# Weights decoded beside the second part's steps, and the mixing's bias copied into PSUM by ScalarE

## The chip, the cores and the metric

One core of a Trainium2 chip. The time is the device time of one execution in microseconds, as the median of several runs of the whole kernel, from x and the weights in HBM to the output in HBM.

## What is computed

x has 4 batches of 3072 tokens with 256 features. The work goes through three layers, cut here to what matters:

```python
X  = rfft(x, axis=1)
Yr = Xr @ w_r - Xi @ w_i + b_r
Yi = Xr @ w_i + Xi @ w_r + b_i
Y  = soft_threshold(Yr, 0.01) + 1j * soft_threshold(Yi, 0.01)
y  = irfft(Y)

h  = y @ w_in                    # 256 -> 2048
z  = (h * tanh(softplus(h))) @ w_out

xk = mu_k * z + (1 - mu_k) * z_prev      # z_prev: the token before
xr = mu_r * z + (1 - mu_r) * z_prev
v  = relu(xk @ w_k) ** 2 @ w_v           # 256 -> 1024 -> 256
out = sigmoid(xr @ w_r2) * v
```

The weights w_in, w_out, w_k, w_v and w_r2 (called w_g in the kernel) arrive as 64-bit floats. The kernel reads each as two 32-bit words and rebuilds a 32-bit value from them, which it then splits into a high and a low part, so that three matmuls (high by high, low by high, high by low) give nearly full precision.

## The kernel before, in words

**The first part** (`part1`) is the transform, the mixing with w_r and w_i, the threshold and the inverse transform. It runs over 48 units, u = 0 to 47: four batches of NT = 12 groups of frequencies, t = u mod 12. A unit's matmuls on TensorE are F(u+1), the transform of the next unit (`emit_F`), M(u), the mixing (`emit_M`), and I(u-1), the inverse of the unit before (`emit_I`). M(u) fills one bank of the PSUM pool psy, which has three buffers: twelve matmuls of 512 columns, and a thirteenth that adds b_r and b_i. That one multiplies the constant tile pick (lines of ones, chosen by partition) by the tile bias. In a unit with t = 0 each of these is done in two halves of 256 columns, so there are 26. ScalarE and VectorE take the results out: `post_F` (a Copy to xh on ScalarE, a subtraction to xl on VectorE), `post_M` (a Relu on ScalarE), `post_M2` (a combined add and min on VectorE), `post_I` (a Copy to bs on ScalarE, and a store to b_dr on SP's queue). Between them VectorE does the butterflies of the long transform. These come from lists that a planner (`Background`) hands out: it adds up estimated costs against a clock, in which a unit is 1710 for F, 2770 for M and 1710 for I, and a list entry can have a unit by which it is due.

**The second part** (`part2`) runs over 24 blocks of 512 tokens with NC = 16 steps each, s = 0 to 383 and some more to drain. Step s has the six matmuls H(s) (`emit_H`, y by w_in, 128 of the 2048 features), a Mish on ScalarE a step later (`act_mish`), on VectorE the high and the low part of the result (`dve_g`, tiles gh and gl), and three steps after H the six matmuls acc(s-3) into the block's sums (`emit_acc`, with w_out). H and the other short-lived results share the PSUM pool psw with four buffers. From step 16 on the third layer of the block before runs in between, by the table PLAN: `evac` (copies of the sums), `token_mix` (one operation on ScalarE and three on VectorE for each half), `emit_K` and `post_K`, `emit_V`, `emit_R` (with a Sigmoid), `finish`. In block 0 the token mix stands at steps 19, 20, 24 and 25, the first K at step 22. Within one step every engine's instructions stand in the order in which the program emits them: on ScalarE the Mish first and then the list ax, on VectorE the two operations of `dve_g` with the list vx pushed between and behind them. An engine takes its own instructions in that order. What is left of the butterflies (`f3_ops`, halves of a batch, each loading a tile g) is put in by F3_PART2 and `Background.one`, a few operations per step.

**Decoding.** A weight comes in 25 pieces of 512 KB: eight of w_in, eight of w_out, four of w_k, four of w_v, one of w_g. A piece is a raw load (`raw_piece`, on SP's queue), then by `decode`: a0 (ScalarE, a Copy to integer and a Sign, into the tile sg), v0 (VectorE, two operations that put the magnitude together, into the tile q), a1 (ScalarE, Abs of q), v1 (VectorE, q by sg), a2 (ScalarE, the high part), v2 (VectorE, the low part; for w_out and w_k a2 and v2 are two operations of half the size). The class `Weights` is a pipeline of four stages: `vec()` moves every piece one stage on and gives v2 of the piece in stage 3, v1 of the one in stage 1 and v0 of the one in stage 0, in this order; `sca()` gives a2 of the piece in stage 2, a0 and a1 of the one in stage 0, and the next raw load. In the first part sg has two buffers, q three, and raw four.

All 25 are decoded in the first part. Five of the nine of w_k, w_v and w_g go through in units 6 to 14; the other 20 pieces in units 36 to 47, two per unit. The nine are parked in HBM (`park_piece`, the tensor w_dr), as their place in SBUF is taken until the second part, which fetches them back at its start (`fetch`, 21 loads on SP's queue).

```python
        def sca(self, depth):
            p = self.pipe
            ops = (p[2][3]() if p[2] else []) + (p[0][0]() + p[0][5]() if p[0] else [])
            return ops + [lambda: self.load(depth)]
```

In the profile most instructions stand under the line of a helper: 155 is `mm`, 152 `act`, 146 `tt`, 149 `stt`. They are told apart by their tiles: yps is M, xps F, bps I, hps H, a acc, kps K, u the result of the Mish.

Of the kernel before, what the change touches and what calls it, by code (L numbers as in the profile page):

```python
# [24 lines left out]
NB = 4  # L25
# [4 lines left out]
NT = 12  # L30
# [6 lines left out]
START = (20500, 20500)  # L37
SLACK = (2000, 3200)

NPARK = 5  # L40
PARK_AT = (6, 15)

F3_PART1 = {(1, 4): [(0, 0)], (1, 8): [(0, 1)]}
F3_PART2 = {1: (1, 0), 3: (1, 1), 5: (2, 0), 8: (2, 1), 10: (3, 0), 14: (3, 1)}


SPLIT_AT = (13, 14)
# [66 lines left out]
def tile_fft_mix_moe_channel_mix(  # L114
# [26 lines left out]
    def emit(ops):  # L141
        for e in ops:
            e()
# [12 lines left out]

    dram = pool(ctx, "dram", 1, space=bass.MemoryType.DRAM)
    b_dr = [dram.tile([2, 128, NT, 256], F32, name=f"b_dr{b}") for b in range(NB)]
    w_dr = [dram.tile([128, 2, 512], F32, name=f"w_dr{i}") for i in range(9)]
    y_dr = [dram.tile([2, 128, 24, 128], F32, name=f"y_dr{b}") for b in range(NB)]  # L160

    cst = pool(ctx, "cst", 1)
# [272 lines left out]

    raws = []

    def raw_piece(src):
        p, tag = raws[1][raws[0] % len(raws[1])]
        raws[0] += 1  # L440
        raw = p.tile([128, 512, 2], I32, tag=tag, name="raw", bufs=2)
        nc.sync.dma_start(out=raw.rearrange("p (k f) t -> p k (f t)", k=2),
                          in_=src.bitcast(I32).rearrange("(k p) f -> p k f", p=128))
        return raw

    def decode(raw, parts, scale=1.0):
        hw, lw = raw[:, :, 1], raw[:, :, 0]
        tl = {}

        def a0():  # L450
            sg = tl["sg"] = pools["st"].tile([128, 512], F32, tag="sg", name="sg")
            return [lambda: act(sg.bitcast(I32), hw.bitcast(F32), ACTF.Copy, scale=14000.0),
                    lambda: act(sg, sg.bitcast(I32), ACTF.Sign)]

        def v0():
            q = tl["q"] = pools["st"].tile([128, 512], F32, tag="q", name="q", bufs=3)
            qi = q.bitcast(I32)
            return [lambda: V.tensor_scalar(out=qi, in0=hw, scalar1=0x08000000, scalar2=3,
                                            op0=ALU.bitwise_xor, op1=ALU.logical_shift_left),
                    lambda: stt(qi, lw, 29, qi, ALU.logical_shift_right, ALU.bitwise_or)]  # L460

        def a1():
            return [lambda: act(tl["q"], tl["q"], ACTF.Abs)]

        def v1():
            return [lambda: stt(tl["q"], tl["q"], 3.4e38, tl["sg"], ALU.min, MULT)]

        def a2():
            tl["p"] = parts(tl["q"])
            return [lambda hi=hi, v=v: act(hi, v, ACTF.Copy, scale=scale) for hi, lo, v in tl["p"]]  # L470

        def v2():
            if scale == 1.0:
                return [lambda hi=hi, lo=lo, v=v: tt(lo, v, hi.bitcast(F32), SUB) for hi, lo, v in tl["p"]]
            return [lambda hi=hi, lo=lo, v=v: stt(lo, v, scale, hi.bitcast(F32), MULT, SUB)
                    for hi, lo, v in tl["p"]]

        return a0, v0, v1, a2, v2, a1

    def win_piece(i):  # L480
        raw = raw_piece(w_in[:, 256 * i:256 * i + 256])
        cs = slice(256 * i, 256 * i + 256)
        w = wt["in"]
        return decode(raw, lambda q: [(w[:, 0, :, cs], w[:, 1, :, cs],
                                q.rearrange("p (k f) -> p k f", k=2))])

    def wout_piece(i):
        raw = raw_piece(w_out[256 * i:256 * i + 256, :])

        def parts(q):  # L490
# [3 lines left out]
        return decode(raw, parts)  # L494


    parked = ([w_k[:, 256 * i:256 * i + 256] for i in range(4)]
              + [w_v[256 * i:256 * i + 256, :] for i in range(4)] + [w_g])

    def park_piece(i):  # L500
        raw = raw_piece(parked[i])
        tl = {}

        def parts(q):
            t = tl["t"] = yhl_p.tile([128, 2, 512], F32R, tag="yl", name="wp")
            return [(t[:, 0, :], t[:, 1, :], q)]
        a0, v0, v1, a2, v2, a1 = decode(raw, parts)
        return a0, v0, v1, a2, lambda: v2() + [lambda: nc.sync.dma_start(out=w_dr[i], in_=tl["t"].bitcast(F32))], a1

    def fetch():  # L510
        for i in range(4):
            nc.sync.dma_start(out=wt["v"][:, :, 2 * i:2 * i + 2, :].bitcast(F32),
                              in_=w_dr[4 + i].rearrange("p s (c f) -> p s c f", c=2))
        nc.sync.dma_start(out=wt["g"].bitcast(F32), in_=w_dr[8].rearrange("p s (c f) -> p s c f", c=2))
        for c in range(8):
            wt["k", c] = mat.tile([128, 2, 2, 128], F32R, tag="m", name="wkt")
            src = w_dr[c // 2].rearrange("p s (h k f) -> p s h k f", h=2, k=2)
            for z in range(2):
                nc.sync.dma_start(out=wt["k", c][:, z].bitcast(F32), in_=src[:, z, :, c % 2, :])

    class Weights:

# [48 lines left out]
    def part1():  # L571
        with ExitStack() as es:
# [11 lines left out]
            fm, im = {}, {}  # L584
            bias = c1.tile([128, 512], F32R, name="bias")
            pick = c1.tile([128, 2, 128], F32R, name="pick")
            zero = c1.tile([128, 64], F32, name="zero")
            As = {}

# [25 lines left out]
            def post_F(u):  # L615
# [7 lines left out]
                if t == 0:  # L623
# [5 lines left out]
                                     in_=zero[:, 0:4].rearrange("p (a o) -> p a o", o=1), func=ACTF.Copy)  # L629
                    xt[u] += (zh, zl)  # L630

            def emit_M(u):
                t = u % NT
                ps = psy.tile([128, 512], F32, tag="y", name="yps")
                xs = xt.pop(u)
                if t:
                    groups = [(slice(0, 512), ((0, 256, 0), (1, 0, 0)))]
# [4 lines left out]
                for gs, parts in groups:  # L642
                    n = gs.stop - gs.start
                    todo = []
                    for zl, lo in ((0, 0), (0, 1), (1, 0)):
                        for h in range(2):
                            w = wt["mix", h][lo]
                            for r, c0, z in parts:
                                todo.append((xs[z + zl][:, h, 128 * r:128 * r + 128], w[:, c0:c0 + n]))
                    todo.append((pick[:, 0 if t else 1, :], bias[:, gs]))  # L650
                    for i, (l, r) in enumerate(todo):
                        mm(ps[:, gs], l, r, i == 0, i == len(todo) - 1)
                yps[u] = ps


            def post_M(u):
# [69 lines left out]
            bg.add(both(z[8:], m[:4]) + m[4:])  # L726
            bg.flush()
            emit_F(0)
            post_F(0)
            bg.add(both(t0[0][1], t0[1][1]) + both(t0[0][2][:10], t0[1][2][:10]), 4)  # L730
            bg.add(both(t0[0][2][10:], t0[1][2][10:]), 8)
# [4 lines left out]
            for u in range(NU):  # L736
# [8 lines left out]
                bg.step()  # L745
                if u == NU - NT - 1:
                    wt["in"] = big.tile([128, 2, 2, 2048], F32R, tag="big", name="win")
                    todo = [lambda: win_piece(0)]
                    for i in range(8):
                        if i < 7:  # L750
                            todo.append(lambda i=i: win_piece(i + 1))
                        todo.append(lambda i=i: wout_piece(i))
                    late = [lambda i=i: park_piece(i) for i in range(NPARK, 9)]
                    wq = Weights(todo[:6] + late + todo[6:])
                    wq.load(3)
                dec = 0
                if b == NB - 1:
                    dec = 2
                elif PARK_AT[0] <= u < PARK_AT[1]:
                    dec = 1  # L760
                    if u == PARK_AT[0]:
                        wq = Weights([lambda i=i: park_piece(i) for i in range(NPARK)])
                        wq.load(2)
                bg.flush(u + 1)
                if u == 6:
                    S.activation(out=mu1, in_=mu, func=ACTF.Copy, scale=-1.0, bias=1.0)
                pe += 1710 * (u + 1 < NU)
                if u + 1 < NU:
                    emit_F(u + 1)
# [14 lines left out]
                    emit(wq.sca(2))  # L784
                if u > 1:
                    post_I(u - 2)
                if dec == 2:
                    emit(wq.vec())
                    emit(wq.sca(2))
                    bg.clock += 2100  # L790
                emit_M(u)
                pe = max(pe, x_at + 300) + 2770
                y_new = pe + 700
                if u:
                    emit_I(u - 1)
# [5 lines left out]
            while wq.busy():  # L801
                emit(wq.vec())
                emit(wq.sca(2))
            for h in range(2):
                emit(split_y(0, h)[1])
            post_M(NU - 1)
            post_M2(NU - 1)
            post_I(NU - 2)
            emit_I(NU - 1)
            post_I(NU - 1)  # L810
# [2 lines left out]
    def part2():  # L813
        with ExitStack() as es:
# [18 lines left out]
            xr = (xr_p.tile([128, 2, 512], F32R, name="xrh"), xr_p.tile([128, 2, 512], F32R, name="xrl"))  # L833
            xs = x2_p.tile([128, 1088], F32, name="x2s")[:, 0:1026].rearrange("p (h f) -> p h f", h=2)

            fetch()
            NC = 16
            h_t, u_t, gh, acc, kt = {}, {}, {}, {}, {}
            vps, rt, mix_t = {}, {}, {}
# [137 lines left out]
            for s in range(max(max(plan), max(fin_at)) + 2):  # L977
                j, c = divmod(s, NC)
                if s < NS:
                    if c == 10 and j + 1 < NBLK:  # L980
                        load_y(j + 1)
                    if j in F3_PART2 and c == 0:
                        bg.jobs.append(F3_PART2[j])
                    bg.step()
                    emit_H(s)
                ax, vx = defer.pop(s, ([], []))
# [12 lines left out]
                    act_mish(s - 1)  # L999
                for e in ax:  # L1000
                    e()
                vx = list(vx)
                bg.have = min(bg.have + FILL[0], FILL[1])

# [62 lines left out]
```

## Time and profile before

| | |
|---|---|
| median of 3 runs | 1982.79 us (1981.26 to 1983.64) |
| the profiled execution | 1981.86 us |
| its span | 1979.9 us |
| around the span | 1.96 us |
| TensorE busy (PE) | 1958.0 us, 99% |
| TensorE's weight loads (PEld) | 1686.2 us, 85% |
| VectorE (DVE) | 1141.4 us, 58% |
| ScalarE (ACT) | 929.0 us, 47% |
| mean granted clock of TensorE | 1.00 |

The first part ends and the second begins at about 327 us of the span. A row of the profile gives the line, the engine, the operation, the tile written and the tiles read; "idle before" is the time in which that engine did nothing ahead of it, and the arrow names what ended it. Matmuls overlap, so the mean duration of one is longer than the distance to the next. SPq rows are transfers issued on SP's queue; their duration is that of the issue.

### The profile page before, as it was taken

The page shows a single profiled execution, that of the slowest core. Times are in us where ns is not written, and L with a number is a line of the kernel's source. Part 1 is how long each engine was busy: PE and PEld are TensorE (multiplying, and loading weights), DVE is VectorE, ACT ScalarE, POOL GpSimd, SP SyncE. Part 2 cuts the span into 40 slices and gives each one's busy share as a digit, 9 for nine tenths or more (in the row PEclk, how much of TensorE's full clock was granted, in tenths as well). Part 3 has the DMA queues.
Part 4 walks back from the last instruction along what each step waited for, and adds up shares of the span by engine and source line. Part 5 has one row for each costly group of instructions (what it writes and reads, how often), then busy time and mean ns, then how long its engine had stood idle before and what let it go on. Part 6 is the DMA issues. An engine that isn't in the chain of part 4 may idle for free.

```text
span 1979.9 us, 25685 instructions
## 1 busy us (share of the span) xinstructions
PE 1958.0 (99%) x10084; PEld 1686.2 (85%) x10084; DVE 1141.4 (58%) x2183; ACT 929.0 (47%) x1525; POOL 13.2 (1%) x28
## 2 busy tenths in 40 slices
PE   6999999999999999999999999999999999999999
PEld 5888888888888888888888888888888888888888
DVE  8999976665654754465375445555544544444444
ACT  2422286344544554454445444444544544454455
POOL 0000000000000000000000000000000000000000
PEclk9999999999999999999999999999999999999999
DMA  9445276111011010101101001011000000000000
GB/s 279 150 138 170 70 245 200 39 32 65 22 33 54 22 44 11 54 22 33 54 22 54 1 22 54 5 33 38 22 1 22 22 11 12 22 23 1 22 11 22
DMA packets 104554, 106.66 MB, mean 54 GB/s; under 512 B 7017, under 2 KB 85489, under 8 KB 103409
## 3 DMA queue, kind: packets, MB, share of 16 engines
q1 hardware_dynamic: 104432, 105.02, 16.7%
q8 instruction: 79, 1.29, 0.3%
q14 instruction: 43, 0.34, 0.1%
HBM read 62.53 MB, written 42.47 MB: 53 GB/s over the span
## 4 chain that ended last, share of the span: by engine, by line
PE 97%; DMA 1%; DVE 1%; ACT 0%; issue 0%; SPq 0%; DVEq 0%; ACTq 0%
PE a L155 26%; PE hps L155 26%; PE v L155 14%; PE kps L155 13%; PE yps L155 7%; PE bps L155 4%; PE xps L155 4%; PE zps L155 3%; DMA a<-in_x_dram 1%; DMA w_dr<-wp 0%; DVE g L146 0%; ACT sg L152 0%; SPq L266 0%; DVE q L149 0%; ACT q L152 0%
## 5 line engine op out<-in xcount | busy, mean ns | idle before, releaser
L863 DVE CAST gh<-u 128x512 fp32r<-128x512 f32 x384 | 163.2, 425 | 747.5 <-PE a L155 598.2
L155 PE MATMUL a<-gh,wo 128*128 128x512 f32 x1536 | 536.3, 390 | 0.0
L155 PE MATMUL hps<-yh,win 128*128 128x512 f32 x1536 | 534.7, 389 | 0.0
L152 ACT ACTIVATE u<-hps 128x512 f32<-128x512 f32 x384 | 229.7, 598 | 525.0 <-PE hps L155 368.8
L155 PEld LDWEIGHTS hps<-yh,win 128*128 128x128 f32 x1536 | 288.3, 188 | 60.3
L155 PEld LDWEIGHTS a<-gh,wo 128*128 128x128 f32 x1536 | 288.4, 188 | 58.0
L155 PE MATMUL a<-gl,wo 128*128 128x512 f32 x768 | 299.9, 390 | 0.0
L155 PE MATMUL hps<-yl,win 128*128 128x512 f32 x768 | 298.8, 389 | 0.0
L155 PE MATMUL kps<-b,wkt 128*128 128x512 f32 x960 | 280.1, 390 | 0.0
L155 PE MATMUL v<-b,kh 128*128 128x256 f32 x1536 | 275.8, 281 | 0.0
L146 DVE TENSOR_TENSOR gl<-u,gh 128x512 fp32r<-128x512 f32 x384 | 263.6, 687 | 3.6
L155 PEld LDWEIGHTS v<-b,kh 128*128 128x128 f32 x1536 | 243.7, 190 | 7.6
L155 PE MATMUL v<-b,kl 128*128 128x256 f32 x768 | 215.8, 281 | 0.0
L155 PEld LDWEIGHTS kps<-b,wkt 128*128 128x128 f32 x960 | 179.1, 188 | 36.1
L152 ACT ACTIVATE ka<-kps 128x512 f32<-128x512 f32 x192 | 115.0, 599 | 185.5 <-PE kps L155 185.5
L155 PEld LDWEIGHTS hps<-yl,win 128*128 128x128 f32 x768 | 144.1, 188 | 29.9
L155 PEld LDWEIGHTS a<-gl,wo 128*128 128x128 f32 x768 | 144.5, 188 | 26.6
L146 DVE TENSOR_TENSOR kl<-ka,kh 128x512 fp32r<-128x512 f32 x192 | 132.5, 690 | 32.8 <-ACT ka L152 19.1
L155 PEld LDWEIGHTS v<-b,kl 128*128 128x128 f32 x768 | 144.1, 188 | 0.0
L152 ACT ACTIVATE ka<-ka 128x512 f32<-128x512 f32 x192 | 121.4, 632 | 6.3
L152 ACT ACTIVATE kh<-ka 128x512 fp32r<-128x512 f32 x192 | 121.4, 632 | 6.3
L146 DVE TENSOR_TENSOR g<-g 128x128 f32<-128x128 f32 (+3 forms) x272 | 107.5, 433 | 1.2
(80 smaller groups left out, 1926.8 us busy)
## 6 DMA issues: line engine op xcount, KB each, us to landing
b_dr<-bs SPq DMA_DIRECT2D x48, 256.0 KB, 2.2
g<-b_dr SPq DMA_DIRECT2D x8, 1536.0 KB, 6.8
y<-y_dr SPq DMA_DIRECT2D x48, 256.0 KB, 3.2
out_dram<-r SPq DMA_DIRECT2D x48, 256.0 KB, 2.2
y_dr<-g SPq DMA_DIRECT2D x80, 64.0 KB, 1.6
w_dr<-wp SPq DMA_DIRECT2D x9, 512.0 KB, 5.9
a<-in_x_dram SPq DMA_DIRECT2D x8, 512.0 KB, 6.2
y_dr<-g SPq DMA_DIRECT2D x32, 128.0 KB, 1.9
```

Source lines behind the costliest of these rows:

```text
L146: V.tensor_tensor(out=o, in0=a, in1=b, op=op)
L152: S.activation(out=o, in_=i, func=f, **kw)
L155: T.matmul(out=o, lhsT=l, rhs=r, start=start, stop=stop, **kw)
L863: return [lambda: V.tensor_copy(hi, u), lambda: tt(lo, u, hi.bitcast(F32), SUB)]
```

## The change

Two things. The weights that were parked are decoded in the second part, together with five pieces of w_out: 14 pieces, one entering at every second step from step 0 on (DEC_STEPS). Their `vec()` goes to the front of that step's list vx, their `sca()` into the next step's list ax. Their working tiles lie in the tile g, which is free there: one slot for sg, three for q, two for raw. The butterfly jobs of batch 1 move from steps 16 and 48 to 34 and 50. In the first part 11 pieces are left, one per unit from unit 34 on. w_dr is gone.

And b_r and b_i are no longer added by a matmul: the bank of M(u+1) is filled at the top of unit u by a ScalarE Copy from one of two SBUF tiles called full, and M's first matmul adds to what is there. The first three units still use a matmul, which now comes ahead of the others. The two tiles full are made once, by two matmuls and two copies behind F(0). At the end of the first part the split of y(0) moves behind post_M2(47). The planner's cost of M falls from 2770 to 2550.

```diff
-NPARK = 5
-PARK_AT = (6, 15)
+NWO = 3
+DEC_STEPS = range(0, 34, 2)
-F3_PART2 = {1: (1, 0), 3: (1, 1), 5: (2, 0), 8: (2, 1), 10: (3, 0), 14: (3, 1)}
+F3_PART2 = {34: (1, 0), 50: (1, 1), 80: (2, 0), 128: (2, 1), 160: (3, 0), 224: (3, 1)}
...
+    def stage(tag, bufs):
+        if "slots" in pools:
+            slots, at = pools["slots"]
+            at[tag] += 1
+            return slots[tag][at[tag] % len(slots[tag])]
+        return pools["st"].tile([128, 512], F32, tag=tag, name=tag, bufs=bufs)
...
-            sg = tl["sg"] = pools["st"].tile([128, 512], F32, tag="sg", name="sg")
+            sg = tl["sg"] = stage("sg", 2)
...
-            q = tl["q"] = pools["st"].tile([128, 512], F32, tag="q", name="q", bufs=3)
+            q = tl["q"] = stage("q", 3)
...
+            def pre_M(u):
+                ps = yps[u] = psy.tile([128, 512], F32, tag="y", name="yps")
+                i = 0 if u % NT else 1
+                if u < 3:
+                    mm(ps, pick[:, i, :], bias, True, False, skip_group_check=True)
+                else:
+                    act(ps, full[i], ACTF.Copy)
...
-                    todo.append((pick[:, 0 if t else 1, :], bias[:, gs]))
                     for i, (l, r) in enumerate(todo):
-                        mm(ps[:, gs], l, r, i == 0, i == len(todo) - 1)
-                yps[u] = ps
+                        mm(ps[:, gs], l, r, False, i == len(todo) - 1, skip_group_check=True)
...
             emit_F(0)
+
+            for i in range(2):
+                ps = psb.tile([128, 512], F32, tag="b", name="cps")
+                mm(ps, pick[:, i, :], bias, True, True)
+                act(full[i], ps, ACTF.Copy)
             post_F(0)
...
+                if u == NU - NT - 3:
+                    wq = Weights([lambda i=i: win_piece(i) for i in range(8)] +
+                                 [lambda i=i: wout_piece(i) for i in range(NWO)])
                     wq.load(3)
...
+                dec = u > NU - NT - 3
                 bg.flush(u + 1)
...
+                if u == 0:
+                    pre_M(0)
+                if u + 1 < NU:
+                    pre_M(u + 1)
                 pe += 1710 * (u + 1 < NU)
...
-                pe = max(pe, x_at + 300) + 2770
+                pe = max(pe, x_at + 300) + 2550
...
+            post_M(NU - 1)
+            post_M2(NU - 1)
             for h in range(2):
                 emit(split_y(0, h)[1])
-            post_M(NU - 1)
-            post_M2(NU - 1)
...
-            fetch()
+            for c in range(8):
+                wt["k", c] = mat.tile([128, 2, 2, 128], F32R, tag="m", name="wkt")
+
+            G = g_p.tile([128, 8, 512], F32, tag="g", name="stage")
+            slots = {"sg": [G[:, 0, :]], "q": [G[:, i, :] for i in (1, 2, 3)],
+                     "raw": [G[:, 4:6, :], G[:, 6:8, :]]}
+            pools["slots"] = (slots, dict.fromkeys(slots, 0))
+            wq = Weights([lambda i=i: wout_piece(i) for i in range(NWO, 8)] +
+                         [lambda i=i: wk_piece(i) for i in range(4)] +
+                         [lambda i=i: wv_piece(i) for i in range(4)] + [wg_piece])
+            wq.load(2)
...
+                if s in DEC_STEPS and wq.busy():
+                    vx = wq.vec() + list(vx)
+                    later(s + 1, wq.sca(2), [])
                 vx = list(vx)
```

wk_piece, wv_piece and wg_piece, which take the place of park_piece, write the two parts straight to the tiles that the matmuls read.

## Rows read from the trace of the kernel before

**Rows 1.** The page, busy time, share of the span and instructions of each engine

```profile
PE 1958.0 (99%) x10084; PEld 1686.2 (85%) x10084; DVE 1141.4 (58%) x2183; ACT 929.0 (47%) x1525; POOL 13.2 (1%) x28
```

**Rows 2.** Table of stretches: length, each engine's busy us, PE's granted clock, DMA

```profile
0.00:20.00 20.00, 2.40 (x7) 1.77 (x8) 11.66 (x23) 4.69 (x10) 0.20 (x4) 1.00 0.93 281
...
290.00:300.00 10.00, 9.74 (x44) 7.91 (x43) 8.63 (x16) 9.90 (x21) 0.00 (x0) 1.00 0.94 314
...
350.00:400.00 50.00, 50.00 (x223) 41.39 (x222) 33.17 (x67) 19.86 (x35) 0.34 (x1) 1.00 0.04 16
```

**Rows 3.** Timeline, ScalarE, an early step of the second part: start, us, what

```profile
346.71 0.60 ACT L152 ACTIVATE u<-hps 128x512 f32<-128x512 f32 x1 [2.12 <-PE hps L155]
```

**Rows 4.** Groups by line and shape, the bias matmul: busy us, mean ns

```profile
L155 PE MATMUL yps<-bias,pick 128*128 128x512 f32 x44 | 17.1, 389 | 0.0
```

**Rows 5.** Timeline, TensorE, a unit's bias matmul and the inverse behind it

```profile
306.21 0.39 PE L155 MATMUL yps<-bias,pick 128*128 128x512 f32 x1
...
306.44 1.89 PE L155 MATMUL bps<-im,yb 128*128 128x256 f32 x8
```

**Rows 6.** Timeline of the start: the bias tile, and TensorE's wait for VectorE

```profile
19.70 0.68 DVE L146 TENSOR_TENSOR bias<-braw,bhi 32x512 fp32r<-32x512 f32 x1
...
21.95 1.35 PEld L155 LDWEIGHTS xps<-fm,g 128*128 128x128 f32 x4 [0.44 <-DVE g L149]
```

**Rows 7.** Groups by line and shape: the pieces, g, the token mix

```profile
L146 DVE TENSOR_TENSOR gl<-u,gh 128x512 fp32r<-128x512 f32 x384 | 263.6, 687 | 3.6
...
L863 DVE CAST gh<-u 128x512 fp32r<-128x512 f32 x384 | 163.2, 425 | 747.5 <-PE a L155 598.2 <-ACT u L152 149.3
...
L149 DVE SCALAR_TENSOR_TENSOR t<-x2s,mu,t 128x512 f32<-128x512 f32 x96 | 71.7, 746 | 7.3 <-ACT t L152 7.3
...
L149 DVE SCALAR_TENSOR_TENSOR q<-raw,q 128x512 int32<-128x512 int32 x25 | 17.3, 693 | 0.9
L149 DVE SCALAR_TENSOR_TENSOR q<-q,sg 128x512 f32<-128x512 f32 x25 | 17.2, 689 | 7.0 <-ACT q L152 6.9
...
L152 ACT ACTIVATE sg<-raw 128x512 int32<-128x512 f32 x25 | 16.6, 666 | 0.0
...
L152 ACT ACTIVATE sg<-sg 128x512 f32<-128x512 int32 x25 | 15.8, 632 | 0.8
...
L152 ACT ACTIVATE q<-q 128x512 f32<-128x512 f32 x25 | 15.4, 615 | 0.1
...
L458 DVE TENSOR_SCALAR q<-raw 128x512 int32<-128x512 int32 x25 | 10.6, 422 | 5.7 <-DMA raw<-in_moe_w_in_dram 3.6 <-DMA raw<-in_moe_w_k_dram 2.1
...
L146 DVE TENSOR_TENSOR wo<-q,wo 128x256 fp32r<-128x256 f32 x16 | 6.0, 417 | 0.0
```

**Rows 8.** Timeline where the second part begins: all engines

```profile
324.78 0.69 DVE L149 SCALAR_TENSOR_TENSOR yb<-yps,yb 128x512 f32<-128x512 f32 x1 [0.94 <-ACT yb L152]
...
327.22 0.58 PE L155 MATMUL hps<-yh,win 128*128 128x512 f32 x1
...
328.73 2.57 SPq L512 DMA_DIRECT2D b<-w_dr  x4
...
332.86 0.39 PE L155 MATMUL a<-gh,wo 128*128 128x512 f32 x1
```

**Rows 9.** The tile raw: its 25 loads, from issue to landing

```profile
DMA to landing us min/median/max: 3.8/5.4/7.1
```

**Rows 10.** ScalarE's table loads: all of them, and one in the timeline

```profile
L152 ACT ACT_TABLE_LOAD x49 | 62.9, 1283 | 10.3 <-DMA braw<-in_b_r_dram 9.4
...
440.24 0.58 ACT L152 ACTIVATE u<-hps 128x512 f32<-128x512 f32 x1
440.84 1.28 ACT L152 ACT_TABLE_LOAD   x1
442.13 1.09 ACT L152 ACTIVATE r<-zps 128x512 f32<-128x512 f32 x2
```

**Rows 11.** Timeline, TensorE, step 22: the first K

```profile
384.54 1.52 PE L155 MATMUL kps<-b,wkt 128*128 128x512 f32 x6
```

More of the change, by code (lines that the diff above doesn't have):

```diff
@@ L158, in tile_fft_mix_moe_channel_mix @@
     b_dr = [dram.tile([2, 128, NT, 256], F32, name=f"b_dr{b}") for b in range(NB)]
-    w_dr = [dram.tile([128, 2, 512], F32, name=f"w_dr{i}") for i in range(9)]
     y_dr = [dram.tile([2, 128, 24, 128], F32, name=f"y_dr{b}") for b in range(NB)]
@@ L436, in tile_fft_mix_moe_channel_mix @@
     raws = []
-    def raw_piece(src):
-        p, tag = raws[1][raws[0] % len(raws[1])]
-        raws[0] += 1
-        raw = p.tile([128, 512, 2], I32, tag=tag, name="raw", bufs=2)
+    def stage(tag, bufs):
[4 more added lines that the diff above has]
+        return pools["st"].tile([128, 512], F32, tag=tag, name=tag, bufs=bufs)
+    def raw_piece(src):
+        if "slots" in pools:
+            raw = stage("raw", 2).bitcast(I32).rearrange("p a f -> p (a f)").rearrange("p (f t) -> p f t", t=2)
+        else:
+            p, tag = raws[1][raws[0] % len(raws[1])]
+            raws[0] += 1
+            raw = p.tile([128, 512, 2], I32, tag=tag, name="raw", bufs=2)
         nc.sync.dma_start(out=raw.rearrange("p (k f) t -> p k (f t)", k=2),
@@ L482, in win_piece @@
         cs = slice(256 * i, 256 * i + 256)
-        w = wt["in"]
-        return decode(raw, lambda q: [(w[:, 0, :, cs], w[:, 1, :, cs],
+        return decode(raw, lambda q: [(wt["in"][:, 0, :, cs], wt["in"][:, 1, :, cs],
                                 q.rearrange("p (k f) -> p k f", k=2))])
@@ L494, in wout_piece, with wk_piece, wv_piece, wg_piece @@
         return decode(raw, parts)
[L497 to L502, printed above, removed]
-        def parts(q):
[L505 to L519, printed above, removed]
+    def wk_piece(i):
+        raw = raw_piece(w_k[:, 256 * i:256 * i + 256])
+        def parts(q):
+            z = q.rearrange("p (k f) -> p k f", k=2)
+            return [(wt["k", 2 * i + c][:, 0, :, :], wt["k", 2 * i + c][:, 1, :, :],
+                     z[:, :, 128 * c:128 * c + 128]) for c in range(2)]
+        return decode(raw, parts)
+    def wv_piece(i):
+        raw = raw_piece(w_v[256 * i:256 * i + 256, :])
+        w = wt["v"][:, :, 2 * i:2 * i + 2, :]
+        return decode(raw, lambda q: [(w[:, 0], w[:, 1], q.rearrange("p (c f) -> p c f", c=2))])
+    def wg_piece():
+        raw = raw_piece(w_g)
+        w = wt["g"]
+        return decode(raw, lambda q: [(w[:, 0], w[:, 1], q.rearrange("p (c f) -> p c f", c=2))])
     class Weights:
@@ L586, in part1 @@
             pick = c1.tile([128, 2, 128], F32R, name="pick")
+            full = [c1.tile([128, 512], F32, name=f"full{i}") for i in range(2)]
             zero = c1.tile([128, 64], F32, name="zero")
@@ L630, in post_F @@
                     xt[u] += (zh, zl)
+            def pre_M(u):
[3 more added lines that the diff above has]
+                    mm(ps, pick[:, i, :], bias, True, False, skip_group_check=True)
+                else:
+                    act(ps, full[i], ACTF.Copy)
             def emit_M(u):
                 t = u % NT
-                ps = psy.tile([128, 512], F32, tag="y", name="yps")
+                ps = yps[u]
                 xs = xt.pop(u)
@@ L747, in part1 @@
                     wt["in"] = big.tile([128, 2, 2, 2048], F32R, tag="big", name="win")
[L748 to L754, printed above, removed]
-                    wq.load(3)
[L756 to L763, printed above, removed]
+                if u == NU - NT - 3:
+                    wq = Weights([lambda i=i: win_piece(i) for i in range(8)] +
+                                 [lambda i=i: wout_piece(i) for i in range(NWO)])
+                    wq.load(3)
+                dec = u > NU - NT - 3
                 bg.flush(u + 1)
@@ L786, in part1 @@
                     post_I(u - 2)
[L787 to L790, printed above, removed]
                 emit_M(u)
-                pe = max(pe, x_at + 300) + 2770
+                pe = max(pe, x_at + 300) + 2550
                 y_new = pe + 700
@@ L981, in part2 @@
                         load_y(j + 1)
-                    if j in F3_PART2 and c == 0:
-                        bg.jobs.append(F3_PART2[j])
+                    if s in F3_PART2:
+                        bg.jobs.append(F3_PART2[s])
                     bg.step()
```

## The prediction

> **What bounds the kernel now.** I read the page's busy shares first, then the table of stretches, then single lines. TensorE is busy 99% of the span [rows 1], and the stretches say where the rest begins: the first 20 us, in which it works 2.40 us, and 0.26 us near 290 us [rows 2]. Inside both parts no stretch is short of matmuls: from 350 to 400 us TensorE has 50.00 of 50 while VectorE has 33.17 and ScalarE 19.86 [rows 2]. So a matmul that goes is worth its issue time, and work on the other two engines costs nothing until something waits for it. ScalarE's Mish shows the second part's pace: 2.12 us idle for the matmuls, then 0.60 of work, one step in 2.72 us [rows 3]. Two steps, the decoding's new unit, are 5.44 us. From these averages 14 pieces look free. The averages hide three things: activation tables, the one buffer for signs, and in-order queues.
>
> **Bias matmuls.** 44 of the 512-column kind [rows 4]; the four units with t = 0 have two halves instead. The bias one starts at 306.21 and the next group at 306.44, so 0.23 us each [rows 5]; the 0.39 mean is pipelined duration. From unit 3 on, 42 units lose a whole one (9.66) and three lose two halves (0.69): 10.35 us. Units 0 to 2 keep theirs ahead of the mixing, and two more are added to make the tiles `full`. Those before F(1) cost nothing: bias is ready at 19.70 + 0.68 = 20.38, and TensorE waits until 21.95 for VectorE's lines anyway [rows 6]. Four of them (0.92) fit into that wait, so units 0 and 1 gain 0.46; from that I take 0.2, because the two copies into `full` stand ahead of xh(0) on ScalarE. Without that wait they would cost 0.92. Sum: 10.6 us gained.
>
> The copy that replaces each matmul is a 128x512 ScalarE operation; nearest is the Mish, 0.60 us [rows 3]. It stands a whole unit ahead of its matmuls. It waits for VectorE's last read of that bank three units back, and behind it stands post_M(u-1), which waits for TensorE anyway. ScalarE is fullest near 290 us, 9.90 of 10 [rows 2], with two pieces per unit; the change leaves one there, which frees some 2.5 us per unit. I take 0; if cover fails, the bound is 0.60 in 45 units, 27 us.
>
> **Fewer pieces in the first part.** 25 become 11. That takes 14 x 2.5 us from VectorE and as much from ScalarE, all beside a full TensorE: worth the 0.26 us hole [rows 2], which is where parked pieces went out. The nine stores and 21 loads of `w_dr` leave SP's queue; the 14 raw loads move to the second part. In the planner 2770 becomes 2550, which follows the shorter unit. With the hole, the first part gives 10.9 us.
>
> The halves of y(0) are now split after post_M2(47) on VectorE. That ends at 324.78 + 0.69 = 325.47; four operations (two of 0.43, two of 0.69) end at 327.7. H(0) starts at 327.22 [rows 8] and wants the last only with its fifth matmul, 4 x 0.23 later, at 328.1. No cost; without the cover, 0.5 us. F3's two jobs move from steps 16 and 48 to 34 and 50; y of batch 1 is wanted at step 90, and VectorE has a third of its time free [rows 2]. I take 0, up to 2 us.
>
> **Decoding in the second part.** Times here are on the old trace's clock. The first raw load stands on SP behind the last b_dr store, where the first fetch stood, 328.73 [rows 8]. It lands 3.8 to 7.1 later, median 5.4 [rows 9]: 334.1. Each later raw load waits on SP for the Copy two pieces before it; the y loads queued behind are wanted only three steps on. Step 0 puts its VectorE operations ahead of g(0), which acc(0) wanted at 332.86 [rows 8]. So the change opens with a wait of some 3 us, and behind it ScalarE's Copy for piece 0 stands ahead of Mish(1).
>
> Then the tables. Before, 49 loads of 1.283 us were one at the start, one for the first Mish and two around the Sigmoids of 23 blocks, one in the last [rows 10]. Sign and Abs ran only before the first Mish; no row shows them under the table that Mish loads. A switch starts 0.02 us after the operation before it ended, and the next starts 0.01 after it [rows 10]. Each piece brings a Sign and Abs between two Mish. Bounds: no switch, or two per piece. I take two, 28 in all: only Copy, Relu and Square are shown beside Mish.
>
> The Trainium skill (ScalarE: Activation LUTs, "What ACT_TABLE_LOAD costs") gives a switch 1283 ns and a drain of 1380 ns; the trace agrees with the first and shows no drain. By the page the sum would be 28 x 1.38 = 39 us higher; I go by the row.
>
> Now a cycle of two steps. From the Copy on, ScalarE has Copy 0.67, load 1.28, Sign 0.63, Abs 0.62, load 1.28: 4.48 us, and only then the next Mish [rows 7, 10]. Signs have one slot, where the first part had two, so this Copy waits for VectorE's product q x sign of the piece before. On VectorE that stands behind g of the odd Mish: Mish 0.60, gh 0.43, product 0.69, and from step 6 on also gl 0.69 and two wo halves of 0.42 [rows 7]. Cycle without the wo halves and gl: 1.72 + 4.48 = 6.20; with them 3.25 + 4.48 = 7.73. Both exceed 5.44.
>
> Chain: Mish(1) at 334.1 + 4.5 = 338.6; two cycles of 6.20 to Mish(5), 351.0; seven of 7.73 to Mish(19), 405.1, plus 0.7 for a token-mix operation before its load: 405.8. Step 20's token mix stands behind Mish 0.60, gh, wo, gl, wo, product (2.65), the next piece's q (0.42 + 0.69) and its own three (0.75, 0.43, 0.69) [rows 7]: 412.0. K(0,0) waits for it and before started at 384.54 [rows 11]: TensorE is 27.5 us late. The last pieces lie beside K and V, where steps are longer; bounds 0 and 3 x 2.29 = 6.9, and I take 1.5, near the low end, as each K adds six matmuls (1.38). Loss: 29.0 us.
>
> Sum against the profiled execution: 1981.86 - 10.9 + 29.0 = 2000.0. The median is 0.93 above it: 2000.9.
>
> **Rivals.** First, faster: Mish's table serves Sign and Abs. What decides is the count of table loads, 49 instead of 77. Then a cycle fits into 5.44 us: 1.92 of Copy, Sign and Abs, two Mish of 0.60, two copies of wo (0.42 each, as on VectorE), and the hold on the Copy makes it 3.25 + 1.92 = 5.17 at most. What stays is the first landing (334.1, q 0.42 + 0.69, g(0) 0.43 + 0.69, less 332.86: 3.4) and the token mix before K(0,0), which stands behind five decode operations on VectorE (2.64) and behind Copy, Sign and Abs on ScalarE (1.92): between 2.64 and 4.56, I take 3.2. Time: 1982.79 - 10.9 + 6.6 = 1978.5. For it: part 1 ran Copy, Relu, Sign and Abs without a switch. Against: no row has them beside Mish. Chance 0.07.
>
> The same page ("Table sets: the hidden batching unit") says that copy, relu and abs are in every set; Sign is not in that list, and no row here shows either after a Mish.
>
> Second, switches that take nothing from TensorE's path beyond ScalarE's own sum: if VectorE's hold on the Copy hid, a cycle would be two Mish, two wo copies and 4.48, about 6.4 instead of 7.73. Nine cycles less 1.3 each: 12 us less, 1989. One sign slot speaks against it. Chance 0.14; it is the range's low end.
>
> Third, a switch that holds ScalarE for as long again as its load lasts: 28 x 1.28 = 36 us more, 2037; the gaps of 0.02 and 0.01 [rows 10] speak against it. Chance 0.02; the page's drain would be this case. Fourth, the new copies on ScalarE hold up the first part: half of 27 us gives 2014. Chance 0.03; part 1 has a unit's lead on each.
>
> **How the numbers follow.** The chain as summed has 0.74, with 1994 to 2011: landing at 7.1 adds 1.7, the last pieces at their full price 5.4, some 3 for handing over. The range reaches down to the second rival, 1988 to 2011, and leaves out the others. A 0.2% change, 4 us, is about what a measurement of this kernel tells from none. Faster 0.06, same 0.03, slower 0.91: the first rival makes nearly all of the first two, and a chain at half its loss the rest.
>
> **What would show it.** Units of the first part 0.23 us shorter, no bias matmuls after unit 2. About 77 table loads, the new ones between Mish(1) and Mish(28). TensorE idle in the stretch after its first Mish by a quarter, waiting for gl and for the token mix, and none after step 36. Table loads at 49 would make it wrong; so would Copy starting before the product. TensorE's clock I leave at 2.4 GHz, the upper of its two levels: it was granted 1.00 even with 2.40 us busy in 20 [rows 2]; a lower figure in the stalled stretch would add time.

## The result and the profile after

The changed kernel takes 1998.99 us (1998.41 to 1999.8), beside 1982.16 of the kernel before: a ratio of 1.0084, 95% interval 1.0069 to 1.0099. The forecast was 2000.9. The profiled execution is 1998.41 us with a span of 1996.2.

One event splits the span so that the change's two halves can be read apart: the start of H(0), TensorE's first matmul of the second part. It was at 327.22 us [rows 8]. After, in TensorE's timeline:

```profile
317.37 0.58 PE L157 MATMUL hps<-yh,win 128*128 128x512 f32 x1
```

So the first part gave 9.85 us. Some of that is chance: TensorE's first matmul, which hangs on the landing of x, came at 16.17 us before and at 15.81 after. From H(0) to the end of the span it was 1979.9 - 327.22 = 1652.7 and is 1996.2 - 317.37 = 1678.8: the second part lost 26.1.

Where it was lost shows in the table of stretches of the changed kernel (length, busy us of TensorE, its weight loads, VectorE, ScalarE and GpSimd, granted clock, DMA):

```profile
20.00:300.00 280.00, 279.02 (x1311) 239.98 (x1311) 238.17 (x493) 127.94 (x240) 0.00 (x0) 1.00 0.43 134
317.40:396.00 78.60, 65.41 (x254) 47.94 (x253) 44.82 (x91) 66.06 (x97) 0.00 (x0) 0.96 0.31 94
396.00:430.00 34.00, 30.55 (x143) 24.55 (x142) 24.76 (x47) 31.33 (x45) 0.70 (x1) 1.00 0.16 47
430.00:1900.00 1470.00, 1470.00 (x7720) 1267.84 (x7719) 769.73 (x1450) 700.59 (x1117) 11.95 (x21) 1.00 0.09 29
```

TensorE is full in the first part but for one hole, idle a sixth of the time while pieces are decoded, and full again from 430 us on. Nothing is made up later: what TensorE loses it keeps. The idle time up to 430 us is 13.2 + 3.4 = 16.6 us of the 26.1. The rest stands as busy: behind a wait the next matmul starts 0.34 us later in the place of 0.23, and for a while the clock is lower (last section).

The groups by line, ScalarE, answer to [rows 10]. There are 28 more table loads, two for each of the 14 pieces:

```profile
L154 ACT ACT_TABLE_LOAD x77 | 98.8, 1283 | 10.6 <-DMA braw<-in_b_r_dram 9.2
```

And ScalarE's timeline shows one cycle of two steps, from Mish(7) to Mish(9). It answers to [rows 3], where a Mish came every 2.72 us. A row "x2" holds two operations of a kind; the tile "stage" is the one with sg, q and raw in it:

```profile
347.31 1.09 ACT L154 ACTIVATE u<-hps 128x512 f32<-128x512 f32 x2
348.28 0.72 ACT L154 ACTIVATE wo<-stage 128x256 fp32r<-128x256 f32 x2
350.32 0.68 ACT L154 ACTIVATE stage<-stage 128x512 int32<-128x512 f32 x1 [1.32 <-issue]
351.01 1.28 ACT L154 ACT_TABLE_LOAD   x1
352.31 1.16 ACT L154 ACTIVATE stage<-stage 128x512 f32<-128x512 int32 x2
353.48 1.28 ACT L154 ACT_TABLE_LOAD   x1
354.77 1.09 ACT L154 ACTIVATE u<-hps 128x512 f32<-128x512 f32 x2
```

Read it downwards: two Mish, the high parts, 1.32 us of waiting, the Copy, a load, Sign and Abs, a load, the next Mish. The cycle is 354.77 - 347.31 = 7.46 us, where TensorE needs 5.44. The trace names "issue" for the wait; VectorE's timeline says what it is, as its product q by sg of the piece before ends at 349.55 + 0.69 = 350.24, 0.08 before the Copy:

```profile
347.94 0.43 DVE L880 CAST gh<-u 128x512 fp32r<-128x512 f32 x1 [3.06 <-ACT u L154]
348.28 0.42 DVE L148 TENSOR_TENSOR wo<-stage,wo 128x256 fp32r<-128x256 f32 x1
348.62 0.69 DVE L148 TENSOR_TENSOR gl<-u,gh 128x512 fp32r<-128x512 f32 x1
349.22 0.42 DVE L148 TENSOR_TENSOR wo<-stage,wo 128x256 fp32r<-128x256 f32 x1
349.55 0.69 DVE L151 SCALAR_TENSOR_TENSOR stage<-stage 128x512 f32<-128x512 f32 x1
```

TensorE's own waits up to 430 us are for the most part for gh and gl (10.9 us); 2.2 are for the token mix at step 22, and 3.4 for the split of y, the copies of the sums and a Mish:

```profile
324.58 0.50 PE L157 MATMUL a<-gh,wo 128*128 128x512 f32 x1 [1.41 <-DVE gh L880]
...
348.42 0.50 PE L157 MATMUL a<-gh,wo 128*128 128x512 f32 x1 [0.69 <-DVE gh L880]
349.36 0.50 PE L157 MATMUL a<-gl,wo 128*128 128x512 f32 x1 [0.43 <-DVE gl L148]
...
398.93 0.51 PE L157 MATMUL kps<-b,wkt 128*128 128x512 f32 x1 [2.00 <-DVE b L912]
```

The first part's hole is near 180 us: the inverse waits for VectorE's yb, which stands behind a butterfly that waits for x of the next batch:

```profile
177.18 2.36 DVE L148 TENSOR_TENSOR a<-a 128x1024 f32<-128x1024 f32 x2 [4.28 <-DMA a<-in_x_dram]
179.46 0.68 DVE L151 SCALAR_TENSOR_TENSOR yb<-yps,yb 128x512 f32<-128x512 f32 x1
...
180.19 1.99 PE L157 MATMUL bps<-im,yb 128*128 128x256 f32 x8 [0.97 <-DVE yb L151]
```

### The profile page after: what moved, and what is told of

The parts are those of the page before. It is cut to its first block, busy times and chain, and to the rows that moved or that the text cites. A ratio compares the mean times of both kernels' runs of the same rounds, so it can differ in the third digit from the quotient of the medians.

```text
span 1996.2 us, 25615 instructions
## 1 busy us (share of the span) xinstructions
PE 1957.2 (98%) x10037; PEld 1678.0 (84%) x10037; DVE 1140.1 (57%) x2187; ACT 989.6 (50%) x1604; POOL 13.6 (1%) x28
## 3 DMA queue, kind: packets, MB, share of 16 engines
q8 instruction: 78, 1.28, 0.3%
## 4 chain that ended last, share of the span: by engine, by line
PE 79%; ACT 0%; DVE 0%; issue 0%; DVEq 0%; ACTq 0%
PE a L157 25%; PE hps L157 24%; PE v L157 13%; PE kps L157 13%; PE zps L157 3%; ACT L154 0%; ACT stage L154 0%; DVE t L151 0%; DVE xkl L148 0%; DVE r L148 0%; ACT x2s L154 0%; ACT ka L154 0%; ACT u L154 0%; DVE b L912 0%; ACT kh L154 0%
```

## The experiments

The theory: two table switches per piece, and the one slot for signs, make a cycle longer than TensorE's two steps; the bias copies cost nothing. Twelve runs test its terms. For each profiled execution the table gives the start of H(0) and the rest of its span, so that the noise of the first part does not blur the second: the hole near 180 us is 0.7 to 2.4 us where it occurs (in the changed kernel and six of the runs), and TensorE's first matmul comes between 15.6 and 17.6 us.

| kernel | median us | ratio, 95% interval | H(0) at | rest of span |
|---|---|---|---|---|
| before | 1982.16 | | 327.22 | 1652.7 |
| changed | 1998.99 | 1.0084 (1.0069 to 1.0099) | 317.37 | 1678.8 |
| no switches | 1977.83 | 0.9979 (0.9970 to 0.9988) | 321.07 | 1658.3 |
| Abs kept | 2001.34, one | | 318.63 | 1680.5 |
| two sign slots | 1988.79 | 1.0032 (1.0019 to 1.0044) | 319.38 | 1669.2 |
| early raw loads | 1996.00 | 1.0070 (1.0055 to 1.0085) | 318.21 | 1675.9 |
| signs by VectorE | 1978.85 | 0.9983 (0.9974 to 0.9992) | 317.87 | 1657.7 |
| the same, early raw loads | 1972.87 | 0.9955 (0.9942 to 0.9967) | 317.04 | 1653.0 |
| the same, later butterflies | 1972.35 | 0.9949 (0.9936 to 0.9963) | 317.83 | 1652.9 |
| decoding moved alone | 2007.76 | 1.0130 (1.0114 to 1.0145) | 326.45 | 1679.0 |
| moved by VectorE's signs, early, bias matmuls | 1981.34 | 0.9997 (0.9988 to 1.0006) | 326.55 | 1652.9 |
| bias copy alone | 1992.95 | 1.0052 (1.0040 to 1.0065) | 335.87 | 1652.7 |
| the same, planner cost 2770 | 1981.26 | 0.9995 (0.9986 to 1.0004) | 326.04 | 1652.7 |
| bias copy alone, copies left out | 1989.80 | 1.0039 (1.0025 to 1.0052) | 333.77 | 1653.2 |

**No switches.**

```diff
-lambda: act(sg, sg.bitcast(I32), ACTF.Sign)]
+lambda: act(sg, sg.bitcast(I32), ACTF.Copy if "slots" in pools else ACTF.Sign)]
...
-return [lambda: act(tl["q"], tl["q"], ACTF.Abs)]
+return [lambda: act(tl["q"], tl["q"], ACTF.Copy if "slots" in pools else ACTF.Abs)]
```

> In the second part Sign and Abs become Copy, so the decoded weights there keep a wrong sign bit; every instruction stays where it is, and ScalarE has as many operations of the same size, but none that needs another table. Theory (the switches set the cycle): 49 table loads instead of 77, a cycle of two steps falls from the 7.47 us between Mish(5) and Mish(7) of the changed kernel to TensorE's 5.44, and of the 26 us that the second part lost 4 to 6 are left (the first landing and the token mix before the first K): 1977 to 1980 us. Rival (the decoding's own operations in the in-order queues are the cause): 77 loads gone but the cycle still over 6 us, 1987 us or more.

49 loads, and ScalarE's timeline has Mish(8) to Mish(10) in TensorE's time, with the same operations between them:

```profile
344.49 0.60 ACT L154 ACTIVATE u<-hps 128x512 f32<-128x512 f32 x1 [2.00 <-PE hps L157]
344.99 0.71 ACT L154 ACTIVATE wo<-stage 128x256 fp32r<-128x256 f32 x2
345.60 1.85 ACT L154 ACTIVATE stage<-stage 128x512 int32<-128x512 f32 x3
347.36 0.58 ACT L154 ACTIVATE u<-hps 128x512 f32<-128x512 f32 x1
349.93 0.60 ACT L154 ACTIVATE u<-hps 128x512 f32<-128x512 f32 x1 [2.00 <-PE hps L157]
```

5.44 us, and ScalarE waits for TensorE again. The second part's loss falls from 26.1 to 5.6. The switches are 20.5 us of it. What is left is 1.8 us of waiting for g(0), 1.1 for the token mix, and a lower clock behind the first wait (granted 0.92 and 0.74 in the five us from 325 and from 330).

**Abs kept.** Of the two, only Sign becomes Copy.

> In the second part Sign alone becomes Copy and Abs stays, so the decoded weights there keep a wrong sign. If Abs is served by the table that serves Mish, 49 table loads and the time of the kernel without switches, 1977 to 1980 us. If it is not, Abs brings the two loads per piece by itself: 77 loads and 1997 to 2000 us. The forecast took the second.

One execution gave 2001.34 us, 1.3 above the range, and the second part loses 27.8. There are 77 loads, and Abs stands alone between two of them:

```profile
344.33 1.35 ACT L154 ACTIVATE stage<-stage 128x512 int32<-128x512 f32 x2 [1.32 <-issue]
345.69 1.28 ACT L154 ACT_TABLE_LOAD   x1
346.99 0.63 ACT L154 ACTIVATE stage<-stage 128x512 f32<-128x512 f32 x1
347.64 1.28 ACT L154 ACT_TABLE_LOAD   x1
```

So Abs alone brings both switches. The Trainium skill (ScalarE: Activation LUTs, "Table sets: the hidden batching unit") lists abs among what every set has; this trace does not agree for Mish's, as the program loads a table before Abs. Whether Mish's table lacks Abs or the load was not needed, no run shows; nor was Sign run without Abs.

**Two sign slots.**

```diff
-slots = {"sg": [G[:, 0, :]], ...
+sg2 = sg_p.tile([128, 4, 256], F32, tag="r", name="sg2")
+slots = {"sg": [G[:, 0, :], sg2[:, 0:2, :].rearrange("p a f -> p (a f)")], ...
```

> The changed kernel with a second slot for the signs, in the tile r that lies idle until step 35. Theory (the Copy waits for VectorE's product because of the one slot): the gap of 1.3 us in front of each Copy goes, the cycle falls from 7.47 to about 6.2 us, which is ScalarE's own sum, and the time by 9 to 12 us, to 1987 to 1990. Rival (ScalarE's own sum sets the cycle and the hold is hidden): the time stays within 2 us of 1999.

The wait before the Copy is gone from ScalarE's timeline, and Mish(7) to Mish(9) is 353.22 - 347.19 = 6.03 us:

```profile
347.19 1.09 ACT L154 ACTIVATE u<-hps 128x512 f32<-128x512 f32 x2
348.16 0.72 ACT L154 ACTIVATE wo<-stage 128x256 fp32r<-128x256 f32 x2
348.78 0.67 ACT L154 ACTIVATE sg<-stage 128x512 int32<-128x512 f32 x1
349.46 1.28 ACT L154 ACT_TABLE_LOAD   x1
350.76 0.63 ACT L154 ACTIVATE sg<-sg 128x512 f32<-128x512 int32 x1
351.29 0.62 ACT L154 ACTIVATE stage<-stage 128x512 f32<-128x512 f32 x1
351.93 1.28 ACT L154 ACT_TABLE_LOAD   x1
353.22 1.09 ACT L154 ACTIVATE u<-hps 128x512 f32<-128x512 f32 x2
```

The loss is 16.5 us: the one slot cost 9.6. It mattered only because the switches had filled ScalarE: in the run without them the one slot is still there, and the cycle is 5.44.

**Early raw loads.** The slots, the pipeline and `wq.load(2)` move from the second part's beginning to the line ahead of post_M(47).

> The changed kernel with the first two raw loads issued ahead of the last two stores of the first part, some 10 us earlier. Theory (ScalarE's chain begins with the landing): the wait before acc(0) goes, every Mish comes 2 to 3 us earlier, and the time falls by 2 to 3 us, to about 1996.3. Rival (a later wait takes up what is gained, such as the token mix before the first K): acc(0) is no longer late but the time stays within 1 us of 1999.

The first raw load is issued 4.7 us ahead of H(0) (313.50 against 318.21) where it was 1.5 behind it, so 6 us earlier and not 10. It gave 1996.0 us, 2.9 less in the second part. TensorE's first wait is now 0.70 us at acc(1); acc(0) has none. The landing was on the path, as the start of a chain that moves as a whole.

**Signs by VectorE.** In the second part one operation on the bits, (hw and sign mask) or q, joins v0, whose first constant changes with it; a0, a1 and v1 give nothing.

```diff
-                    lambda: stt(qi, lw, 29, qi, ALU.logical_shift_right, ALU.bitwise_or)]
+                    lambda: stt(qi, lw, 29, qi, ALU.logical_shift_right, ALU.bitwise_or)] + (
+                [lambda: stt(qi, hw, -2147483648, qi, ALU.bitwise_and, ALU.bitwise_or)] if "slots" in pools else [])
...
```

> The changed kernel, but in the second part the sign is put in by one VectorE operation on the bits (a mask and an or), in the place of the product, and ScalarE's Copy, Sign and Abs are gone; VectorE has as many operations as before. Theory (the switches are the cause): 49 table loads, ScalarE's share of a cycle is two Mish and the high parts, and only the first landing and the token mix before the first K are left: 1975 to 1979 us. Rival (VectorE's four operations per piece, ahead of nothing but in its queue, hold gl and so acc): 1985 or more.

49 loads; the second part loses 5.0 us. Its only waits are at the start: TensorE waits 2.33 and 0.29 us for g(0), and the granted clock is 0.57 in the stretch from 328 to 332 us behind that wait:

```profile
328.00:332.00 4.00, 4.00 (x12) 3.10 (x12) 3.93 (x9) 1.69 (x4) 0.00 (x0) 0.57 0.57 177
```

**The same with early raw loads.**

> Signs by VectorE and the first two raw loads issued ahead of the last two stores of the first part. Theory: without the first landing's wait 2 to 3 us less than with the signs by VectorE alone, 1972.5 to 1976 us; if nothing is late before the first K either, the gain of the bias copy alone, 1972 us. Rival: the wait moves to the token mix, and the time is that with the signs by VectorE alone.

1972.87 us, faster than both kernels. From H(0) on TensorE has no idle row until 420 us; the rest of the span is 1653.0, the kernel before's 1652.7. The token mix before the first K, which the forecast of the first rival had kept at 3.2 us, is not late here.

**The same with later butterflies.** F1_AT is (4, 1, 2, 0) in the place of (4, 1, 1, 0).

> Signs by VectorE, early raw loads, and the butterflies of batch 3 one unit later (F1_AT 2 in the place of 1), when its x has landed. Theory: the hole of 0.93 us near 180 us goes, in which the inverse waits for VectorE, which waits for the x load: 1971.5 to 1972.3 us against 1972.87. Rival: the same butterflies then press on their due unit, and the time is the same or more.

The hole near 180 us is gone (125.00 of 125 us busy from 125 to 250), yet the median is only 0.5 us lower, and H(0) in the profiled execution 0.8 later. That execution started later: its first matmul is at 17.59 us, where the run above has 15.72. From the first matmul to H(0) it is 300.24 us, where it was 301.32. So the trace has the hole's time gained; the medians, whose intervals overlap, do not show it.

**Decoding moved alone.** The changed kernel with the thirteenth matmul back, no copies, and 2770.

> The changed kernel with the bias matmuls of before: only the decoding is moved. Theory (the two parts add): the second part loses the same 26 us and the first gains only the small hole, 2008 to 2009 us. Rival (the shorter units are what pushes the second part's start into waits): the loss falls by some us, 2004 or less.

The second part loses 26.3 us, the first gains 0.8. So the second part's loss is there without the bias copy.

**Decoding moved without its cost, bias matmuls kept.**

> Signs by VectorE and early raw loads in the second part, with the bias matmuls of before. Theory (moved so, the decoding costs TensorE nothing and gains nothing by itself, and only makes room for the bias copies): 1981 to 1983 us, ratio 0.9995 to 1.0005. Rival (the move itself brings part of the 9 us): 1978 or less.

1981.34, within its interval no change. So of the 9 us that the same version with the bias copy gains (1972.87), the move brings none by itself.

**Bias copy alone.** The kernel before with `pre_M`, `full` and 2550, all pieces in the first part.

> The kernel before with the bias copied into PSUM a step ahead and nothing else changed: all pieces decoded in the first part as before. Theory: 10.3 us of matmuls go and 0.3 at the start; the hole near 290 us stays, and ScalarE, with two pieces per unit in the last batch, takes 0.60 us more per unit there: 1971.5 to 1973 us, ratio 0.9945 to 0.9953. Rival (the copies hold up the units where ScalarE is nearly full, 290 to 300 us): 0.6 us lost again in up to twelve units, 1976 to 1979.

This expectation fell, by 20 us: 1992.95 us, slower than before. H(0) is at 335.87 where 316.6 was expected, and TensorE's timeline has holes all through the last batch, each ended by VectorE's yb; three of them, and the last and longest:

```profile
283.81 1.99 PE L155 MATMUL bps<-im,yb 128*128 128x256 f32 x8 [1.36 <-DVE yb L149]
290.60 1.99 PE L155 MATMUL bps<-im,yb 128*128 128x256 f32 x8 [0.29 <-DVE yb L149]
297.92 1.99 PE L155 MATMUL bps<-im,yb 128*128 128x256 f32 x8 [0.86 <-DVE yb L149]
...
332.78 3.44 PE L155 MATMUL bps<-im,yb 128*128 128x256 f32 x8 [6.12 <-DVE yb L149]
```

The 6.12 us are told by VectorE's timeline: yb(47) stands behind the split of y(0), and that waits for its load, which came late behind the last butterflies' stores. Behind the wait the granted clock is 0.50 from 330 to 335 us. Here the split still has its old place, ahead of yb(47); the change has it behind post_M2(47), which keeps such a wait off yb:

```profile
329.13 0.43 DVE L568 CAST yh<-y 128x512 fp32r<-128x512 f32 x1 [4.58 <-DMA y<-y_dr]
...
332.04 0.68 DVE L149 SCALAR_TENSOR_TENSOR yb<-yps,yb 128x512 f32<-128x512 f32 x1
```

**What of this is the planner's.** The same kernel with 2770 in the place of 2550.

> The kernel with the bias copy alone, with the planner's cost of the mixing left at 2770. Theory (ScalarE's time and its order, not the planner): within 3 us of the 1993 that 2550 gave. Rival (the planner's smaller clock moved VectorE's work so that it came late): back to 1972 to 1976.

The rival's cause holds for the larger part, but not its range: 1981.26, 11.7 us less than with 2550 and still 10 above 1971.5. With 2550 VectorE's butterflies come later and meet the two pieces per unit. The stretches from 290 to 300 us, first with 2550 and then with 2770, have VectorE at 9.83 and 9.07 of 10:

```profile
290.00:300.00 10.00, 8.84 (x40) 7.06 (x39) 9.83 (x21) 9.29 (x19) 0.00 (x0) 1.00 0.68 235
...
290.00:300.00 10.00, 8.65 (x38) 7.03 (x38) 9.07 (x17) 9.90 (x21) 0.00 (x0) 1.00 0.83 288
```

With 2550 the load of y(0) is issued at 326.20, behind the last butterflies' stores, and with 2770 at 318.35; TensorE's last wait falls from 6.12 to 0.58 us, and all its waits for yb from 14.3 to 4.7. So part of the 11.7 us is the split's old place, which the change does not have. ScalarE is now at 9.90 of 10; that the copies make the rest is not shown.

**What of it is the copies'.** With 2550 and no bias at all from unit 3 on (b_r and b_i are left out).

> The kernel with the bias copy alone, but the copies are left out too: from unit 3 on nothing adds b_r and b_i, and the first matmul of the mixing starts its bank. All 25 pieces are decoded in the first part. It tells what of the 19 us that the bias copy alone lost against its matmuls is the copies' and what the shorter unit's. Theory (0.6 us of ScalarE per unit, in units where it was full): without them the last batch needs about 6.3 us of ScalarE in a unit of 6.19, so some 1 to 3 us remain lost, and the time is 1972 to 1975. Rival (the shorter units alone leave the two pieces per unit no room): 1983 or more.

The theory fell and the rival holds: 1989.80. Leaving out the copies gives only 3.2 us, and TensorE still waits 13.3 us for yb, 6.0 of them at the end. So with 2550 nearly all of the loss is there without the copies: the shorter unit, with VectorE's work handed out later, is what had no room for two pieces. Of the 21.4 us above 1971.5 the planner's cost is 11.7 with the copies, and the copies are 3.2 with 2550; these need not add, and how the rest splits between the copies, the shorter unit and the place of the split is open. The planner's old cost without copies was not tried, nor the bias copy alone with the split moved, nor the changed kernel with 2770.

## Why the prediction was right

**Bias matmuls, 10.6 us, and the hole, 0.26.** Together 10.9; measured 9.85, and 9.49 if both are counted from TensorE's first matmul. Of the 1.4 then missing, 0.97 is the new hole near 180 us, which no step had: VectorE reached the butterflies of the last batch before their x had landed. It takes both halves of the change, as neither the decoding nor the bias copy alone has a hole there. Without it (later butterflies) the same count gives 311.05 - 300.24 = 10.8. The rest lies at the start: the first inverse begins 16.09 us behind the first matmul (31.90 - 15.81) and before 15.83 (32.00 - 16.17), so 0.26 were lost where the step had 0.46 - 0.2 = 0.26 gained. The unit in the last batch is 303.46 - 297.27 = 6.19 us from inverse to inverse; before it was 306.44 - 300.03 = 6.41.

**Copies at nothing.** Right in the changed kernel, and the cover was named rightly: pieces that had left ScalarE's fullest units. What the step did not see is how much hung on that. It costed each part against a full TensorE as if they added. They do not: the bias copy alone is +10.9 us (1992.95 less 1982.01, the kernel before beside those runs), the decoding alone +25.8, both +16.8. So the bias copy gains some 9 us beside the moved decoding and loses 10.9 without it. Not all of these 20 us is the room that the pieces left: the bias copy alone has the split of y(0) in its old place, and with the planner's old cost it is -0.9 (1981.26 less 1982.12), a difference of 8. What is shown is that it did not pay alone, in either form. "In the planner 2770 becomes 2550, which follows the shorter unit" went in without a price; with two pieces per unit and the split's old place it is worth 11.7 us.

**The landing.** Predicted 6.9 us after H(0), measured 322.98 - 317.37 = 5.6 for the first Copy: the median landing was taken, and this one was quicker. That mis-sized the term by 1.3.

**The switches.** 28, with no drain: the second load's end and the next Mish are 0.01 apart (353.48 + 1.28 = 354.76, and 354.77). Of its two bounds, no switch or two per piece, the prediction took the right one, and the run without switches gives the price, 20.5 us.

**The cycle.** 6.20 and 7.73 predicted, 6.19 (327.43 to 333.62) and 7.46 measured. The 0.27 per cycle is overlap: VectorE's operations of 0.69 start 0.60 apart, as the rows above show, and the sum took whole durations. From Mish(5) to Mish(19) (339.82 to 393.26) it was 53.4 us, where the sum had 54.8. Mish(19) came 75.9 us after H(0), for 78.6: half of the 2.7 is the landing's, half the overlap's, and together they are nearly all that the loss of 29.0 is above the 26.1 measured.

**The first K.** It was late for the reason given, the token mix behind five decode operations on VectorE; three of its six matmuls ran before the wait, as they need only the first half. **The last pieces**, put at 1.5 us: the matmul behind K(0,0) came 24.2 us late (400.24 - 317.37 against 385.90 - 327.22), so 1.9 came behind it.

**What was luck.** The gain was put 1.0 us too high and the loss 2.9 too high, and the two errors partly cancel in the 1.9 by which 2000.9 missed. Of TensorE's clock the prediction took nothing off, and it fell (last section); that hid behind ScalarE's chain. As a sign it named TensorE idle by a quarter of that stretch, and it was a sixth.

**The rivals.** No switch: excluded by 77 loads; made to hold by the run with Copy, it gave 1977.8, where 1978.5 was worked out. The number fits better than its terms: the first landing cost 1.8 us for 3.4 and the token mix 1.1 for 3.2, and about 1.7 of lower clock stood in no term. VectorE's hold hidden: excluded by the 1.32 us; the run with two slots gave 1988.8 for 1989. That too is partly luck: the cycle named there adds up to 1.20 + 0.84 + 4.48 = 6.52 and not 6.4, only seven of the nine cycles are of 7.73, and by these the time would be 1992; the cycle measured 6.03. The drain: excluded. The copies holding up the first part: not in this kernel; in the bias copy alone they are worth 3.2 us of its loss.

## What to carry to other kernels

Before work is moved beside another stage of an in-order engine, ask what it switches there, not only how long it is: 1.9 us of Copy, Sign and Abs fitted easily, and the two table loads that they brought did not. Count in cycles of the waiting chain (who holds the one buffer, what stands ahead in the queue), because the busy share of ScalarE in the stalled stretch is 84% and of VectorE 57%, and neither shows the cycle. And when a change has two halves, price each half with the other absent: here one is a loss alone, the other did not pay alone, and the version with both and without the switches is 0.45% faster than the kernel before.

## What the runs showed that was not expected

TensorE's granted clock fell within the stalled stretch, in which the forecast had left it at its upper level. In the changed kernel's table of stretches:

```profile
364.00:368.00 4.00, 2.99 (x12) 2.17 (x12) 2.54 (x6) 2.72 (x4) 0.00 (x0) 1.00 0.13 33
368.00:372.00 4.00, 1.71 (x6) 1.43 (x7) 2.44 (x5) 3.97 (x7) 0.00 (x0) 0.92 0.28 98
372.00:376.00 4.00, 2.76 (x7) 1.65 (x7) 3.82 (x8) 3.17 (x6) 0.00 (x0) 0.50 0.12 12
376.00:380.00 4.00, 4.00 (x15) 3.18 (x14) 1.68 (x5) 3.35 (x6) 0.00 (x0) 0.73 0.31 119
380.00:384.00 4.00, 4.00 (x19) 3.32 (x18) 2.68 (x6) 3.25 (x5) 0.00 (x0) 1.00 0.30 56
```

After a wait of 3.02 us for gl that ended at 370.29, matmuls start 0.42 apart in the place of 0.23 from 371.3 to about 378: 1.2 GHz, then 2.4 again. It cost little there, since ScalarE's chain was the longer: Mish(13) to Mish(15) is 377.69 - 370.22 = 7.47 us, as in other cycles. In the kernel with the signs by VectorE nothing else was late, and the wait was paid for twice: 2.6 us of waiting for g(0), and then (1 - 0.57) x 4 = 1.7 us at the lower clock, of the 5.0 that it lost. The length of a wait alone does not tell whether the clock falls: behind the hole of 1.90 us near 180 us in the kernel without switches it was 0.74 from 180 to 185 us, and behind that of 2.36 us in the kernel with two sign slots it stayed at 1.00.
